# A ring of nine weight buffers and one of ten for weight sums, the mask on VectorE, a short unit in two PSUM banks, and the first wide group prepared inside the gates

## The chip, the cores and the metric

The kernel runs on one NeuronCore of a Trainium2 chip. The metric is the device time of one execution in microseconds (us). The core's engines each work through a queue of their own in program order: TensorE (PE in the rows, PEld for its weight loads), VectorE (DVE), ScalarE (ACT), GpSimd (POOL) and SyncE (SP), which issues most DMAs. An engine waits on semaphores where an instruction needs another engine's result, and everything behind that instruction on its queue waits with it.

## The reference

Three stages in float32 run after one another on 2304 tokens of width 512:

```
x = windowed_attention(q, k, v)          # 4 batches, 8 heads, 576 positions, window 64
# mixture of experts: 8 experts, hidden width 1024, the two best of each token
for e in range(8):
    for k in range(2):
        mask = top2[:, k] == e
        h = maximum(x[mask] @ w1[e], 0)
        out[mask] += top2_w[mask, k] * (h @ w2[e])
# second feed-forward network, hidden width 2048
h = x @ w_in
g = where(h >= 1, h, where(h <= -1, 0, (h + 1)**2 / 4))
return g @ w_out
```

The weights `w_in` and `w_out` of the last stage arrive as float64 and are turned into float32 on the chip.

## The kernel before

Attention and routing fill the span up to about 108 us. Then come the units of the mixture: expert 0 for all its tokens in two units (0a, 0b), experts 1 to 6 (units e1 to e6, up to 640 rows each, gathered by rank), a short unit "sp" of at most 64 rows of overflow for the last expert (513 to 534 us), and expert 7 in two units (7a, 7b). The last stage has a plain group of two token blocks (g0, 582 to 629 us) and four wide groups of four blocks, which use a Winograd scheme of seven products in place of eight.

TensorE runs one list of steps. A step (ui, f) of unit ui handles chunk f of eight: `do_mm1` of the next chunk (hidden layer, two PSUM banks, split in two parts) and `do_mm2` of its own (output layer, five banks). Every fp32 product is made of three products of a high and a low part, so each weight chunk is split: ScalarE copies the high part (`split_w`, L160), VectorE subtracts it (L161). The hidden layer leaves PSUM through ScalarE (`he`, L876) and VectorE (L879), and the next chunk's products wait until VectorE has read that bank.

Between these operations, units e1 to e6 decode the weights of the last stage. `dec_load` brings one of 32 pieces of float64, `dec_a` makes a mask of its zeros on ScalarE (L185 to L187), and `dec_b` builds float32 on VectorE (L199 to L204) and ends on GpSimd (add L206, multiplication with the mask L207). For every four pieces `sums` builds the eight weight operands of the Winograd scheme: four sums on GpSimd (L224), and eight splits by ScalarE (L240) and VectorE (L241), which then go back to DRAM (w1o). The work of `sums` is put on the list `todo` as four items, and each step takes one item. At the end of each unit GpSimd also issues five scatters of the unit's result rows (L910) and, step by step, the gathers of the next unit's rows (L840).

The short unit computes its hidden layer in one bank: four chunks, a Relu on ScalarE over them (`mm1_half`, L974), four more chunks, a second Relu.

In g0 the hidden layer goes through `act_gate`: r = Relu(h + 1) and then m = min(r/2, 1), (r - m) * m, which is the gate function. Step p of g0 has two gates, (p, 0) and (p, 1); the products of step p + 1 write the same two banks and wait for r of step p. Functions placed on `fill` run inside a gate, behind r. While g0 runs, the rows of the first wide group are read back (`prep_gather`), mixed (`prep_mix`, L1032 and L1034), transposed and copied (`xcopy`, L1232 and L1236), summed (`xsums`, L1246) and split (`xsplit`, L1255 and L1256), at places (p, j) that the last loop lists by hand, where j counts sevenths of a step's output products.

Of the kernel before, what the change touches and what calls it, by code (L numbers as in the profile page):

```python
# [33 lines left out]
RING = 10  # L34
PAIRS = (0, 1, 3, 5)
# [22 lines left out]
def fused_kernel(ctx, tc, qT, kT, v, wg, noise, wcat, out, wd=None):  # L58
# [71 lines left out]
    def stream(k, shape, dt, name):  # L130
        return ring.tile(shape, dt, tag="w", name=name) if k < 2 else pool["we"].tile(shape, dt, tag=f"w{k}", name=name)
# [21 lines left out]
    def split_w(n, half=None):  # L153
        if SP <= n < NCE:
            return
        if half in (None, 0):
            halves[n] = ring.tile([P, 2, 1024], F32R, tag="w", name=f"w{n}")
# [22 lines left out]
    def dec_a(i):  # L180
# [6 lines left out]
        nc.scalar.activation(m, m, AF.Relu)  # L187
        d64[i] = (d64[i], m)

    def dec_b(i):  # L190
        if wd is None:
            t = d64.pop(i)
        else:
# [8 lines left out]
                                           op1=ALU.bitwise_or)  # L202
            nc.vector.tensor_scalar(out=ti, in0=hw, scalar1=-0x800000, scalar2=None, op0=ALU.bitwise_and)
# [3 lines left out]
            nc.gpsimd.tensor_tensor(out=t, in0=t, in1=m, op=ALU.mult)  # L207
# [10 lines left out]
    def sums(p, ta, tb):  # L218
# [27 lines left out]
        todo.extend((lambda: (first(), cut(0, 1)), lambda: (second(), cut(5, 2)), lambda: cut(3, 6), lambda: cut(4, 7)))  # L246
# [522 lines left out]
    dec, xpc = ExitStack(), ExitStack()  # L769
# [192 lines left out]
    def mm1_half(un, n):  # L962
        f, hf = n - SP, NF // 2
        ps = un["m1"][0]
# [37 lines left out]
    unit("sp", E, 0, 1, SP, NF, None, (0,), (2, 3))  # L1002
# [97 lines left out]
    wi, wo = [], []  # L1100
# [30 lines left out]
    def plain(ui, p):  # L1131
        w = wi[p % WS]
        for f in range(2):
# [4 lines left out]
            key = units[ui]["key"]  # L1138
            mm1_of(key, n, units[ui]["T"], act_gate, units[ui]["m1"], part(0), part(1))
# [70 lines left out]
    slots, staged = [], {}  # L1210
# [15 lines left out]
    def xcopy(ui, b):  # L1226
        un = units[ui]
        t = gat.pop((un["key"], b))
        free = [x for x in bank[2:7] if x not in units[ui - 1]["m2"]]
        TR = bank[7] if b % 2 == 0 else free[b // 2 % len(free)]  # L1230
        for k in range(4):
            nc.tensor.transpose(TR[:, k * P:k * P + P], t[:, k * P:k * P + P], idn)  # L1232
        if b == 0:
# [3 lines left out]
                             TR.rearrange("p (o k t) -> p o k t", o=2, k=2), AF.Copy)  # L1237

    def xsums(ui):
        f, d = staged[ui]  # L1240
        if d:
            slots.extend(raw.tile([P, 2, 2, HT], F32R, tag="raw", name=f"xa{i}") for i in range(3))
        t1, t2, t3, t4 = d or [pool["sc"].tile([P, 2, HT], F32, tag="s", name=f"xd{ui}_{i}") for i in range(4)]
# [3 lines left out]
        staged[ui] = (b11, b21, t2, t3, t4, t1, b22)  # L1247
# [25 lines left out]
    for s in range(len(seq)):  # L1273
# [5 lines left out]
        decode = 1 < ui < E - 1 and f <= 6  # L1279
        if ui == 1 and f > 5:  # L1280
            dec_load(ndl)
            ndl += 1
# [8 lines left out]
        if ui == 1 and f == 2:  # L1291
            for x, k in (("rd", 3), ("td", 4), ("so", 6)):
                pool[x] = dec.enter_context(tc.tile_pool(name=x, bufs=k, reuse_waits="tile"))
# [65 lines left out]
        if ui == SPILL - 1 and f == 2:  # L1359
# [86 lines left out]
```

## Time and profile before

| what | value |
|---|---|
| median of 3 runs | 987.42 us (986.65 to 991.91) |
| profiled execution | 988.92 us, of which the span of the profile is 986.9 us |
| TensorE busy | 949.9 us, 96% of the span |
| VectorE, ScalarE, GpSimd busy | 653.2, 461.3, 271.9 us |
| mean granted clock of TensorE | 0.986 of full speed |

A row of the trace gives the start, the duration, the engine, the line of the kernel and the tiles that an operation writes and reads. Where an engine stood idle before it, the row ends in brackets with the idle time and the operation that ended it.

### The profile page before, as it was taken

The page shows a single profiled execution, that of the slowest core. Times are in us where ns is not written, and L with a number is a line of the kernel's source. Part 1 is how long each engine was busy: PE and PEld are TensorE (multiplying, and loading weights), DVE is VectorE, ACT ScalarE, POOL GpSimd, SP SyncE. Part 2 cuts the span into 40 slices and gives each one's busy share as a digit, 9 for nine tenths or more (in the row PEclk, how much of TensorE's full clock was granted, in tenths as well). Part 3 has the DMA queues.
Part 4 walks back from the last instruction along what each step waited for, and adds up shares of the span by engine and source line. Part 5 has one row for each costly group of instructions (what it writes and reads, how often), then busy time and mean ns, then how long its engine had stood idle before and what let it go on. Part 6 is the DMA issues. An engine that isn't in the chain of part 4 may idle for free. (4 is left out here: it accounts for less than half of the span.)

```text
span 986.9 us, 18441 instructions
## 1 busy us (share of the span) xinstructions
PE 949.9 (96%) x6918; PEld 841.7 (85%) x6918; DVE 653.2 (66%) x1358; ACT 461.3 (47%) x938; POOL 271.9 (28%) x303
## 2 busy tenths in 40 slices
PE   8998799999999999799998999899999999999998
PEld 6887789998898888698886888798899899889996
DVE  4689476576786978676442267776766777576664
ACT  6987224566566666554332254344334333433222
POOL 3221113456557676643401020112101201210000
PEclk9999999999999999999998999899999999999999
DMA  8874126568667787777736367484567458556531
GB/s 258 279 243 158 54 97 202 178 231 273 247 232 252 267 287 248 236 229 231 264 108 215 113 206 269 149 304 155 167 225 250 162 173 299 170 171 211 183 117 43
DMA packets 92796, 201.17 MB, mean 204 GB/s; under 512 B 7432, under 2 KB 17928, under 8 KB 92704
## 3 DMA queue, kind: packets, MB, share of 16 engines
q1 hardware_dynamic: 85264, 177.84, 54.1%
q0 software_dynamic: 6144, 19.76, 5.6%
q10 hardware_dynamic: 1296, 2.36, 0.6%
q8 instruction: 55, 0.90, 0.4%
q14 instruction: 37, 0.30, 0.1%
HBM read 159.65 MB, written 40.29 MB: 203 GB/s over the span
## 5 line engine op out<-in xcount | busy, mean ns | idle before, releaser
L931 PE MATMUL bank<-wo,hg 128*128 128x512 f32 x864 | 238.8, 395 | 0.0
L931 PE MATMUL bank<-w,he 128*128 128x512 f32 (+3 forms) x696 | 170.3, 396 | 0.0
L931 PEld LDWEIGHTS bank<-wo,hg 128*128 128x128 f32 x864 | 147.4, 189 | 17.2
L931 PEld LDWEIGHTS bank<-w,he 128*128 128x128 f32 (+3 forms) x696 | 124.7, 184 | 26.6
L868 PE MATMUL bank<-xhie,w 128*128 128x288 f32 (+4 forms) x768 | 123.9, 304 | 9.1 <-DVE he L879 9.0
L868 PEld LDWEIGHTS bank<-xhie,w 128*128 128x128 f32 x768 | 114.5, 192 | 16.6 <-DVE he L879 11.7
L161 DVE TENSOR_TENSOR w<-raw,w 128x1024 fp32r<-128x1024 f32 (+1 forms) x71 | 95.0, 1338 | 39.1 <-ACT w L160 37.0
L876 ACT ACTIVATE he<-bank 128x288 fp32r<-128x288 f32 (+4 forms) x96 | 40.2, 420 | 132.2 <-PE bank L868 129.7
L1176 PEld LDWEIGHTS bank<-xb,wi 128*128 128x128 f32 x576 | 82.2, 192 | 13.8 <-ACT r L886 4.2
L1176 PE MATMUL bank<-xb,wi 128*128 128x256 f32 x576 | 86.7, 287 | 3.8 <-ACT r L886 3.5
L1200 ACT ACTIVATE hg<-cg 128x512 fp32r<-128x512 f32 x64 | 40.3, 629 | 100.5 <-DVE cg L1198 100.5
L1037 POOL TENSOR_TENSOR y<-y,y 128x512 f32<-128x512 f32 x14 | 19.1, 1364 | 200.0 <-ACT y L1036 191.2
L1176 PEld LDWEIGHTS bank<-xc,wi 128*128 128x128 f32 x480 | 67.2, 188 | 7.6 <-DVE wg L1161 0.6
L1176 PE MATMUL bank<-xc,wi 128*128 128x256 f32 x480 | 70.2, 281 | 0.2 <-DVE wg L1161 0.2
L160 ACT ACTIVATE w<-raw 128x1024 fp32r<-128x1024 f32 (+1 forms) x71 | 69.3, 976 | 0.0
L868 PE MATMUL bank<-xloe,w 128*128 128x288 f32 (+4 forms) x384 | 69.2, 303 | 0.0
L879 DVE SCALAR_TENSOR_TENSOR he<-bank,he 128x320 fp32r<-128x320 f32 (+8 forms) x120 | 43.4, 400 | 31.4 <-ACT he L876 26.6
L1194 ACT ACTIVATE mg<-cg 128x512 f32<-128x512 f32 x64 | 40.1, 626 | 48.1 <-DVE cg L1166 46.3
L206 POOL TENSOR_TENSOR td<-rawd 128x512 f32<-128x512 f32 x32 | 33.3, 1042 | 94.9 <-DVE rawd L204 86.3
L1195 DVE SCALAR_TENSOR_TENSOR cg<-mg,cg 128x512 f32<-128x512 f32 x64 | 47.0, 734 | 18.8 <-ACT mg L1194 18.8
L868 PEld LDWEIGHTS bank<-xloe,w 128*128 128x128 f32 x384 | 58.6, 192 | 0.0
L1204 DVE SCALAR_TENSOR_TENSOR hg<-cg,hg 128x512 fp32r<-128x512 f32 x64 | 46.0, 718 | 9.1 <-ACT hg L1200 8.7
(302 smaller groups left out, 1635.1 us busy)
## 6 DMA issues: line engine op xcount, KB each, us to landing
wi<-w1o SPq DMA_DIRECT2D x56, 1024.0 KB
raw<-wcat SPq DMA_DIRECT2D x64, 512.0 KB
rawd<-wd SPq DMA_DIRECT2D x32, 512.0 KB
w1o<-so SPq DMA_DIRECT2D x64, 256.0 KB
y<-y_dram SPq DMA_DIRECT2D x30, 256.0 KB
vE<-v SPq DMA_DIRECT2D x18, 260.0 KB
x_dram<-x SPq DMA_DIRECT2D x18, 256.0 KB
k<-kT SPq DMA_DIRECT2D x8, 512.0 KB
```

The lines of the kernel that those rows point to most:

```text
L160: nc.scalar.activation(w[:, 0, c], t[:, c], AF.Copy)
L161: nc.vector.tensor_tensor(out=w[:, 1, c], in0=t[:, c], in1=w[:, 0, c].bitcast(F32), op=ALU.subtract)
L206: nc.gpsimd.tensor_tensor(out=t, in0=hf, in1=lf, op=ALU.add)
L868: nc.tensor.matmul(ps, lhsT=l[k], rhs=r[:, k, s:s + w], start=(c == 0), stop=(c == len(prods) - 1))
L876: nc.scalar.activation(hh, ps, AF.Relu)
L879: nc.vector.scalar_tensor_tensor(out=t, in0=ps[:, c], scalar=0.0, in1=hh[:, c].bitcast(F32), op0=ALU.max, op1=ALU.subtract)
L931: nc.tensor.matmul(M2[b][0:w], lhsT=h2[:, o:o + w], rhs=r[n], start=(first and a == 0), stop=(last and a == end))
L1176: nc.tensor.matmul(ps, lhsT=w[:, l, k * P:k * P + P], rhs=r[:, m, k, :], start=(c == 0), stop=(c == len(prods) - 1))
L1194: nc.scalar.activation(st["m"], c, AF.Relu, scale=0.5)
L1195: nc.vector.scalar_tensor_tensor(out=c, in0=st["m"], scalar=1.0, in1=c, op0=ALU.min, op1=ALU.subtract)
L1200: nc.scalar.activation(h2[:, 0:T], c, AF.Copy, scale=-1.0)
L1204: nc.vector.scalar_tensor_tensor(out=h2[:, T:2 * T], in0=c, scalar=-1.0, in1=h2[:, 0:T].bitcast(F32), op0=ALU.mult, op1=ALU.subtract)
```

## The change

The ring of split weights gets nine buffers in place of ten (the last chunk of the first expert, and one more of the later weight tiles, get places of their own), and the decode pieces are spread over the steps by a new rule. The four GpSimd sums of four pieces are issued in one item of `todo`; ScalarE and VectorE split in that item and in the next only operands that need no sum, and the summed ones two and three items behind; the buffers for it grow from six to ten. ScalarE's Relu and GpSimd's multiplication for the mask become one VectorE operation in the middle of `dec_b`. The short unit's first half leaves its bank through VectorE, and the second half has a bank of its own. `act_gate` makes half of r on ScalarE and uses combined VectorE operations; and the first wide group's mixing, copies, sums and splits move from the loop into the gates of g0.

```diff
-RING = 10
-PAIRS = (0, 1, 3, 5)
+RING = 9
+PAIRS = (0, 2, 3, 5)
+DEC = 6
...
         nc.scalar.activation(m, m, AF.Sign, bias=tiny[:, 0:1])
-        nc.scalar.activation(m, m, AF.Relu)
...
+            nc.vector.scalar_tensor_tensor(out=hf, in0=m, scalar=0.0, in1=hf, op0=ALU.max, op1=ALU.mult)
             nc.vector.tensor_scalar(out=ti, in0=hw, scalar1=-0x800000, scalar2=None, op0=ALU.bitwise_and)
...
             nc.gpsimd.tensor_tensor(out=t, in0=hf, in1=lf, op=ALU.add)
-            nc.gpsimd.tensor_tensor(out=t, in0=t, in1=m, op=ALU.mult)
...
-        todo.extend((lambda: (first(), cut(0, 1)), lambda: (second(), cut(5, 2)), lambda: cut(3, 6), lambda: cut(4, 7)))
+        todo.extend((lambda: (first(), second(), cut(0, 1)), lambda: cut(4, 7), lambda: cut(5, 2), lambda: cut(3, 6)))
...
         nc.scalar.activation(r, ps, AF.Relu, bias=1.0)
+        nc.scalar.activation(m, r, AF.Copy, scale=0.5)
         while fill:
             fill.popleft()()
-        nc.vector.tensor_scalar(out=m, in0=r, scalar1=0.5, scalar2=1.0, op0=ALU.mult, op1=ALU.min)
-        nc.vector.tensor_tensor(out=r, in0=r, in1=m, op=ALU.subtract)
-        nc.vector.tensor_tensor(out=r, in0=r, in1=m, op=ALU.mult)
-        nc.scalar.activation(hh, r, AF.Copy)
-        nc.vector.tensor_tensor(out=hl, in0=r, in1=hh.bitcast(F32), op=ALU.subtract)
+        nc.vector.scalar_tensor_tensor(out=r, in0=m, scalar=1.0, in1=r, op0=ALU.min, op1=ALU.subtract)
+        nc.vector.scalar_tensor_tensor(out=r, in0=m, scalar=1.0, in1=r, op0=ALU.min, op1=ALU.mult)
+        nc.scalar.activation(hh, r, AF.Copy, scale=-1.0)
+        nc.vector.scalar_tensor_tensor(out=hl, in0=r, scalar=-1.0, in1=hh.bitcast(F32), op0=ALU.mult, op1=ALU.subtract)
...
-        ps = un["m1"][0]
+        ps = un["m1"][f // hf]
...
-            nc.scalar.activation(hbuf["sp"][:, sl], ps[:, sl], AF.Relu)
+            if f < hf:
+                nc.vector.tensor_scalar(out=hbuf["sp"][:, sl], in0=ps[:, sl], scalar1=0.0, scalar2=None, op0=ALU.max)
+            else:
+                nc.scalar.activation(hbuf["sp"][:, sl], ps[:, sl], AF.Relu)
...
-        for out, x, y, e in ((t1, b12, b11, d), (t2, b22, t1, d), (t3, b22, b12, None), (t4, b21, t2, None)):
-            (nc.vector if e else nc.gpsimd).tensor_tensor(out=out, in0=x, in1=y, op=ALU.subtract)
...
+            (nc.vector if d else nc.gpsimd).tensor_tensor(out=out, in0=x, in1=y, op=ALU.subtract)
...
-        decode = 1 < ui < E - 1 and f <= 6
+        decode = 1 < ui < E - 1 and f < DEC and (ui, f) != (2, 0) or (ui, f) in ((2, 6), (2, 7), (3, 6))
...
+    FILL.update({(3, 0): [later(prep_mix, units[g1], b) for b in (0, 1)],
+                 (3, 1): [later(prep_mix, units[g1], b) for b in (2, 3)],
+                 (4, 0): [later(xcopy, g1, b) for b in (0, 1)],
+                 (4, 1): [later(xsplit, g1, 0)],
+                 (5, 0): [later(xsums, g1, (0, 1)), later(xsplit, g1, 1)],
+                 (5, 1): [later(xsums, g1, (2, 3))],
+                 (6, 0): [later(xsplit, g1, j) for j in (2, 3)],
+                 (6, 1): [later(xsplit, g1, j) for j in (4, 5)]})
```

The order of the products on TensorE stays as it was but for the first wide group's transposes. On GpSimd the sums move ahead of the scatters. The rows below are GpSimd's queue around the change from unit e4 to e5 in the kernel before: L206 and L207 end a decode, L910 are the scatters of e4's rows, L224 the sums.

```order
219 L224 TENSOR_TENSOR so_5_5232<-td_5162 128x256
220 L224 TENSOR_TENSOR so_2_5234<-so_5_5232,td_5009 128x256
221 L206 TENSOR_TENSOR td_5242<-rawd_5018 128x512
222 L207 TENSOR_TENSOR td_5242<-td_5242,dm_5203 128x512
223 L910 DMA y_dram<-ye_0_5282,rank_i 23040x512
...
227 L910 DMA y_dram<-ye_4_5309,rank_i 23040x512
228 L224 TENSOR_TENSOR so_3_5332<-td_5009,td_5162 128x256
229 L224 TENSOR_TENSOR so_6_5334<-td_5009,so_2_5234 128x256
230 L840 DMA xge_0_5344<-x_dram,rank_i 128x512
```

The same place in the changed kernel (L207 is its add that ends a decode, L911 its scatters):

```order
191 L911 DMA y_dram<-ye_0_5222,rank_i 23040x512
...
195 L911 DMA y_dram<-ye_4_5249,rank_i 23040x512
196 L841 DMA xge_0_5273<-x_dram,rank_i 128x512
197 L207 TENSOR_TENSOR td_5327<-rawd_4979 128x512
198 L841 DMA xge_1_5336<-x_dram,rank_i 128x512
199 L224 TENSOR_TENSOR so_5_5390<-td_5327 128x256
200 L224 TENSOR_TENSOR so_2_5392<-so_5_5390,td_5047 128x256
201 L224 TENSOR_TENSOR so_3_5394<-td_5047,td_5327 128x256
202 L224 TENSOR_TENSOR so_6_5396<-td_5047,so_2_5392 128x256
```

The four sums now stand together, with no scatters between them. VectorE reaches their splits two items later: the rows below are its queue in the changed kernel after those sums (L162 subtracts a split weight, L241 splits the operands, L199 to L205 decode a piece, L203 being the new operation with the mask).

```order
681 L162 TENSOR_TENSOR w_5473<-raw_5325,w_5473 128x1024
682 L241 TENSOR_TENSOR so_4_5478<-td_5327,so_4_5478 128x256
683 L241 TENSOR_TENSOR so_7_5481<-td_5327,so_7_5481 128x256
684 L199 TENSOR_SCALAR td_5484<-rawd_5271 128x512
685 L201 SCALAR_TENSOR_TENSOR rawd_5271<-rawd_5271,td_5484 128x512
686 L203 SCALAR_TENSOR_TENSOR rawd_5271<-dm_5448,rawd_5271 128x512
687 L204 TENSOR_SCALAR td_5484<-rawd_5271 128x512
688 L205 SCALAR_TENSOR_TENSOR rawd_5271<-rawd_5271,td_5484 128x512
...
694 L241 TENSOR_TENSOR so_5_5390<-so_5_5390 128x256
695 L241 TENSOR_TENSOR so_2_5392<-so_2_5392 128x256
```

Two splits that read only decoded pieces (td) stand ahead of the first two that read sums.

In g0, VectorE's queue in the kernel before holds five splits for the first wide group (L1256) between the gates of step 6 and of step 7 (L889 to L893 are one gate):

```order
865 L889 TENSOR_SCALAR m<-r 128x256
866 L890 TENSOR_TENSOR r<-r,m 128x256
867 L891 TENSOR_TENSOR r<-r,m 128x256
868 L893 TENSOR_TENSOR hg_85_7459<-r,hg_85_7459 128x256
869 L1256 TENSOR_TENSOR xb_7337<-xlos,xb_7337 128x512
870 L1256 TENSOR_TENSOR xb_7338<-xlos,xb_7338 128x512
871 L1256 TENSOR_TENSOR xa_7425<-xlos,xa_7425 128x512
872 L1256 TENSOR_TENSOR xa_7426<-xlos,xa_7426 128x512
873 L1256 TENSOR_TENSOR xa_7427<-xhis,xa_7427 128x512
874 L889 TENSOR_SCALAR m<-r 128x256
```

In the changed kernel (L891 to L894 are a gate's VectorE operations, L1269 the splits, L1258 the sums) the same stretch reads:

```order
879 L1258 TENSOR_TENSOR xlos<-xhis 128x512
880 L1258 TENSOR_TENSOR xlos<-xhis,xlos 128x512
881 L891 SCALAR_TENSOR_TENSOR r<-m,r 128x256
882 L892 SCALAR_TENSOR_TENSOR r<-m,r 128x256
883 L894 SCALAR_TENSOR_TENSOR hg_83_7374<-r,hg_83_7374 128x256
884 L1269 TENSOR_TENSOR xb_7290<-xlos,xb_7290 128x512
885 L1269 TENSOR_TENSOR xb_7291<-xlos,xb_7291 128x512
886 L891 SCALAR_TENSOR_TENSOR r<-m,r 128x256
887 L892 SCALAR_TENSOR_TENSOR r<-m,r 128x256
888 L894 SCALAR_TENSOR_TENSOR hg_84_7410<-r,hg_84_7410 128x256
889 L1269 TENSOR_TENSOR xa_7363<-xlos,xa_7363 128x512
890 L1269 TENSOR_TENSOR xa_7364<-xlos,xa_7364 128x512
```

Each gate now has its share of the preparation in front of its own VectorE operations.

## Rows read from the trace of the kernel before

**Rows 1.** The page: busy time, share of the span, instructions of two engines.

```profile
PE 949.9 (96%) x6918; PEld 841.7 (85%) x6918; DVE 653.2 (66%) x1358; ACT 461.3 (47%) x938; POOL 271.9 (28%) x303
```

**Rows 2.** Stretches of the span: engines' busy us, granted clock, DMA share, GB/s.

```profile
240.00:260.00 20.00, 17.68 (x94) 15.88 (x94) 13.57 (x20) 10.16 (x20) 13.60 (x12) 0.91 0.72 235
380.00:390.00 10.00, 8.79 (x58) 7.78 (x57) 7.87 (x15) 5.36 (x12) 6.97 (x6) 1.00 0.87 281
410.00:430.00 20.00, 14.78 (x73) 13.14 (x73) 8.53 (x19) 8.81 (x16) 10.94 (x11) 0.83 0.74 250
510.00:530.00 20.00, 15.26 (x176) 12.30 (x176) 6.00 (x9) 5.62 (x10) 5.21 (x5) 0.83 0.16 59
600.00:610.00 10.00, 10.00 (x67) 9.01 (x66) 7.43 (x18) 4.14 (x12) 0.00 (x0) 1.00 1.01 356
620.00:640.00 20.00, 16.30 (x89) 14.28 (x89) 13.80 (x29) 5.98 (x14) 1.48 (x2) 0.83 0.39 133
183.00:470.00 287.00, 277.78 (x1624) 249.16 (x1623) 217.62 (x364) 169.77 (x316) 166.74 (x143) 0.98 0.72 242
```

**Rows 3.** Waits of PE from 109 to 990 us: total, times, longest.

```profile
PE bank L868 <- DVE he L879: 9.0, 4, 5.2
PE bank L970 <- ACT hsp L974: 4.6, 1, 4.6
```

**Rows 4.** Timeline around 413 us, change from unit e4 to e5.

```profile
408.96 2.25 POOL L910 DMA_INDIRECT y_dram<-ye,rank_i  x1
...
416.95 0.73 POOL L224 TENSOR_TENSOR so<-td,so 128x256 f32<-128x256 f32 x1
...
417.72 0.42 DVE L241 TENSOR_TENSOR so<-so 128x256 fp32r<-128x256 f32 x1 [7.42 <-POOL so L224]
...
418.57 2.29 PE L868 MATMUL bank<-xhie,w 128*128 128x288 f32 x8 [5.22 <-DVE he L879]
```

**Rows 5.** Waits of DVE from 183 to 470 us: total, times, longest.

```profile
DVE so L241 <- POOL so L224: 20.5, 9, 7.4
```

**Rows 6.** Single lines of DVE and POOL from 183 to 470 us: ns minimum, median, maximum, or busy us and mean ns.

```profile
L161 DVE TENSOR_TENSOR w<-raw,w x40: 1206/1500/2291, 183.2 to 469.6; 128x1024 fp32r<-128x1024 f32 x40
...
L204 DVE SCALAR_TENSOR_TENSOR rawd<-rawd,td x32: 693/694/696, 185.9 to 446.3; 128x512 f32<-128x512 uint32 x32
...
L207 POOL TENSOR_TENSOR td<-td,dm 128x512 f32<-128x512 f32 x32 | 42.3, 1323 | 2.5
```

**Rows 7.** Timeline of the short unit.

```profile
518.11 1.62 PE L970 MATMUL bank<-xsp,w 128*64 128x64 f32 x48
...
519.79 1.23 DVE L161 TENSOR_TENSOR w<-raw,w 128x1024 fp32r<-128x1024 f32 x1 [0.27 <-issue]
...
523.87 0.38 ACT L974 ACTIVATE hsp<-bank 128x256 f32<-128x256 f32 x1 [4.12 <-remote]
...
524.31 3.68 PE L970 MATMUL bank<-xsp,w 128*64 128x64 f32 x64 [4.58 <-ACT hsp L974]
```

**Rows 8.** Timeline of g0 up to the first wide products.

```profile
597.87 0.37 ACT L886 ACTIVATE r<-bank 128x256 f32<-128x256 f32 x1
...
600.04 0.39 ACT L886 ACTIVATE r<-bank 128x256 f32<-128x256 f32 x1
...
604.19 1.32 ACT L1032 ACTIVATE y<-y,wts 128x512 f32<-128x512 f32 x2
...
604.93 1.42 DVE L1034 SCALAR_TENSOR_TENSOR y<-y,wts 128x512 f32<-128x512 f32 x2 [0.19 <-ACT y L1032]
...
620.77 0.69 DVE L1246 TENSOR_TENSOR xlos<-xhis,xlos 128x512 f32<-128x512 f32 x1
...
627.82 1.29 DVE L1256 TENSOR_TENSOR xa<-xlos,xa 128x512 fp32r<-128x512 f32 x2
...
628.57 0.36 ACT L886 ACTIVATE r<-bank 128x256 f32<-128x256 f32 x1
...
628.98 1.65 PE L1176 MATMUL bank<-xb,wi 128*128 128x256 f32 x6 [2.95 <-ACT r L886]
```

More of the change, by code (lines that the diff above doesn't have):

```diff
@@ L1224, in xset, with xturn, xcopy @@
         staged[ui] = (f, d)
-    def xcopy(ui, b):
+    held = {}
+    def xturn(ui, b):
         un = units[ui]
         t = gat.pop((un["key"], b))
-        free = [x for x in bank[2:7] if x not in units[ui - 1]["m2"]]
-        TR = bank[7] if b % 2 == 0 else free[b // 2 % len(free)]
+        free = [bank[7]] + [x for x in bank[2:7] if x not in units[ui - 1]["m2"]]
+        held[ui, b] = to = free[b % len(free)]
         for k in range(4):
-            nc.tensor.transpose(TR[:, k * P:k * P + P], t[:, k * P:k * P + P], idn)
+            nc.tensor.transpose(to[:, k * P:k * P + P], t[:, k * P:k * P + P], idn)
+    def xcopy(ui, b):
         if b == 0:
@@ L1236, in xcopy, with xsums @@
         nc.scalar.activation(staged[ui][0][:, h:h + 2, :, at:at + P],
-                             TR.rearrange("p (o k t) -> p o k t", o=2, k=2), AF.Copy)
-    def xsums(ui):
+                             held.pop((ui, b)).rearrange("p (o k t) -> p o k t", o=2, k=2), AF.Copy)
+    def xsums(ui, part=(0, 1, 2, 3)):
         f, d = staged[ui]
-        if d:
+        if d and 0 in part:
             slots.extend(raw.tile([P, 2, 2, HT], F32R, tag="raw", name=f"xa{i}") for i in range(3))
-        t1, t2, t3, t4 = d or [pool["sc"].tile([P, 2, HT], F32, tag="s", name=f"xd{ui}_{i}") for i in range(4)]
+        if 0 in part:
+            parts[ui] = d or [pool["sc"].tile([P, 2, HT], F32, tag="s", name=f"xd{ui}_{i}") for i in range(4)]
+        t1, t2, t3, t4 = parts[ui]
         b11, b21, b12, b22 = (f[:, i] for i in range(4))
-        for out, x, y, e in ((t1, b12, b11, d), (t2, b22, t1, d), (t3, b22, b12, None), (t4, b21, t2, None)):
-            (nc.vector if e else nc.gpsimd).tensor_tensor(out=out, in0=x, in1=y, op=ALU.subtract)
-        staged[ui] = (b11, b21, t2, t3, t4, t1, b22)
+        for i in part:
+            out, x, y = ((t1, b12, b11), (t2, b22, t1), (t3, b22, b12), (t4, b21, t2))[i]
+            (nc.vector if d else nc.gpsimd).tensor_tensor(out=out, in0=x, in1=y, op=ALU.subtract)
+        if 3 in part:
+            staged[ui] = (b11, b21, t2, t3, t4, t1, b22)
     def xsplit(ui, j):
@@ L1278, in fused_kernel @@
         last = f == len(un["ch"]) - 1
-        decode = 1 < ui < E - 1 and f <= 6
-        if ui == 1 and f > 5:
-            dec_load(ndl)
-            ndl += 1
+        decode = 1 < ui < E - 1 and f < DEC and (ui, f) != (2, 0) or (ui, f) in ((2, 6), (2, 7), (3, 6))
+        if ui == 2 and f == 0:
+            w7.close()
+            for x, k in (("rd", 3), ("td", 4), ("so", 10)):
+                pool[x] = dec.enter_context(tc.tile_pool(name=x, bufs=k, reuse_waits="tile"))
+            for _ in range(2):
+                dec_load(ndl)
+                ndl += 1
         if decode and ndl < n64:
@@ L1290, in fused_kernel @@
             choice_weights()
-        if ui == 1 and f == 2:
-            for x, k in (("rd", 3), ("td", 4), ("so", 6)):
-                pool[x] = dec.enter_context(tc.tile_pool(name=x, bufs=k, reuse_waits="tile"))
+        if ui == SPILL - 1 and f == 2:
+            assert not todo and not stores
+            dec.close()
+            pool["we"] = ffn.enter_context(tc.tile_pool(name="we", bufs=1, reuse_waits="tile"))
         if ui == U7A and f == 0:
@@ L1400, in fused_kernel @@
                     prep_gather(nxt, 2 * p + j)
[L1401 to L1404 removed]
+                if not late:
+                    if 1 <= p < 3 and j in (2, 4):
+                        prep_mix(nxt, 2 * (p - 1) + j // 2 - 1)
+                    if 2 <= p < 4 and j in (1, 3):
+                        xturn(ui + 1, 2 * (p - 2) + j // 2)
+                        xcopy(ui + 1, 2 * (p - 2) + j // 2)
+                elif (p, j) in ((2, 5), (2, 6), (3, 0), (3, 1)):
+                    xturn(ui + 1, 2 * (p - 2) + (j - 5 if p == 2 else j))
+                elif p == 3 and j in (3, 4):
+                    xcopy(ui + 1, j - 1)
                 for x in AT[late].get((p, j), ()):
```

27 lines of the change are left out of this document (12 added, 15 removed).

## Prediction

> **What bounds the kernel now.** I read the page first: TensorE is busy for 949.9 of 986.9 us [rows 1]. What is left to gain is its 37 us of idle time and the stretches in which its clock is low. The change leaves TensorE's products as they are, so I price only those two things. Next I read stretch by stretch [rows 2]. The reader is to see that idle time and low clock come together: 240 to 260 (2.3 us idle, clock 0.91), 410 to 430 (5.2 idle, 0.83), 510 to 530 (4.7 idle, 0.83), 620 to 640 (3.7 idle, 0.83). Then I read TensorE's waits [rows 3]: 9.0 us in four waits for VectorE's `he`, and 4.6 us in one for the short unit's Relu. Attention's own idle time, before 109 us, is untouched.
>
> **Sums behind scatters.** The timeline shows the largest wait from its root [rows 4]. GpSimd begins five scatters at 408.96; the sums queued behind them end at about 417.7; VectorE has stood idle for 7.42 us for the first split of a sum; `he` stands behind that split, and TensorE waits 5.22 us for `he`. In the decode units VectorE waits so nine times, 20.5 us in all [rows 5]. In the change GpSimd does all four sums in one run, and the splits of summed operands come two and three steps later; a step is about 7 us (287 us for 40 splits of weights, one in a step [rows 2, 6]). Against that stands the time of scatters and sums, 417.7 - 408.96 = 8.7 us. I went through the eight groups of pieces in the new order: wherever a split could still meet the scatters in time, it is one that reads decoded pieces alone. So of the 9.0 us I take out the waits of 5.22 us [rows 4], 2.32 (240 to 260) and 1.21 (380 to 390 [rows 2]), behind each of which VectorE stands idle for such a sum: **-8.75**. The fourth, 0.25, stays.
>
> With them goes the low clock. [...] In the second stretch part of the low time lay inside the wait itself, where it costs nothing; I take 2.7 there and 1.7 in the first: **-4.4**. Bounds: 0, if the waits stay, and 5.2.
>
> **Mask on VectorE.** One more operation of 128x512 with two inputs, like L204 (0.694 us), 32 times: +22.2 us of VectorE. GpSimd loses 42.3 us (L207), ScalarE a Relu [rows 6]. From 183 to 470 VectorE is busy for 217.6 of 287 us [rows 2]; with the new operation it would be 239.8, or 84%. That mean hides the full steps: I add up what VectorE has to do in a step with a decode, splits and a transposed block and come to about 6.6 us now and 7.3 us then, an estimate, against a step's 7.2, less in the units with fewer rows. A step that runs over borrows from the next; only when about 4 us have been borrowed does TensorE wait (an estimate: more than half of a step's products lie between a chunk's `he` and the next need of its bank). Six decode steps in a row at 0.5 over borrow 3 us, and two steps without a decode give it back. So I charge **+0.5**; bounds 0 and +9 (rivals).
>
> One thing makes VectorE cheaper again: L161 takes 1.21 us at its shortest and 1.50 in the median, up to 2.29, in the stretch in which GpSimd computes [rows 6]. [...]
>
> **Ring of nine, pieces spread.** With nine buffers a split takes the slot of a chunk whose last product precedes products that the same engine waits for anyway; no wait is added. Loads of pieces move by a step on SyncE's queue and have a step of slack. 0.
>
> **Short unit.** ScalarE's Relu on the first half starts at 523.87, and the second half's 64 products follow at 524.31, after a wait of 4.58 us, because they write the same bank [rows 7]. With a bank of its own the second half starts at once. VectorE's eviction stands behind L161, which ends at about 521.0, so hsp is ready at 521.4, while 64 products of 34 ns (48 in 1.62) run until 521.9: hidden. Gain 4.58 of wait. At full clock the 64 products take 2.2 us instead of 3.68, 1.5 less, and the following ones about 0.7: 2.2 of the 3.4 that the clock row would allow [rows 2, 7]. Less 0.5 for handing over: **-6.3**. One thing is unexplained: the last product of the first half should be done by about 519.8, and yet ScalarE got its signal only at 523.8. If VectorE gets it as late, the output products wait for hsp until 524.2, about 2.3 us. Bounds -2.5 and -7.2.
>
> **Gates.** A gate takes 2.03 to 2.17 us from r to r now (597.87 to 600.04 [rows 8]), and TensorE does not wait but for the last: r of step 7 comes at 628.57 and the wide products wait 2.95. In the change a gate has as many operations in a row as before (m on ScalarE, two on VectorE, hg), so I take 2.1. But what is filled in stands behind r and ahead of the gate's own VectorE operations, and hg and the next r stand behind those. From r of gate (3, 0), 600.04, to r of gate (7, 0) there are eight gates: 16.8 us. The fills add VectorE's work: four mixings of 0.71, four sums of 0.69, six splits of 0.65, 9.5 us in all [rows 8]; and ScalarE's part ahead of it, about 0.65 in each of five fills, 3.3, and handoffs of about 0.1, 1.2 together: 14. Mixing blocks 2 and 3 inside gate (3, 1) also comes some 6 us earlier than now, while the DMA engines are full (share 1.01 in 600 to 610 [rows 2]): up to 1.5 us of waiting for the loads, half of it taken. Sum: 600.04 + 16.8 + 14 + 0.8 = 631.6, against 628.57 now, **+3.0**. TensorE has no work to put there: its own list ends where it ends now. The low clock at 628 to 636 stays. What it gains is one less contended sum (the other three take 0.69 when GpSimd does none). Bounds: -6.4, if all fills are hidden, and +5.
>
> **Sum.** -8.75 - 4.4 + 0.5 - 6.3 + 3.0 = -15.95. From the profiled execution, 988.92, that is 973.0; it lies 1.5 above the median of the runs, so **971.5**. Its own range is 967 to 977.
>
> **The rivals.**
>
> (a) The fills are hidden: what the gates wait for overlaps more than I allow. Then 2.95 and 0.75 of waits and 2.7 of clock go, -6.4 instead of +3.0: 962. Against it: all of it is on two queues in program order.
>
> (b) The short unit's signal is late again: 3.8 of the 6.3 are not gained, 975.3.
>
> (c) VectorE becomes the bound of the decode units. The stretches in which it is nearly full already speak for it. If a step runs 1 us over, six borrow 6, 2 more than the 4 that are free; over the five units 9 us, in waits spread too thin to lower the clock: 980.
>
> (d) Slower than before: the new operation is held up by GpSimd's sums and adds each time, by a whole 1.0 us beside its 0.69. A step is then 1.7 over, six borrow 10, TensorE waits 6 in each of five units, 30 us, less what is gained: 971.5 + 30 = 1001. The point from which this decides is a step 1.4 us longer than TensorE's. Against it: L204 at 693 to 696 ns next to it [rows 6].
>
> (e) The split does not do what it says, since GpSimd is late by more than two steps: 13 us stay, 984.
>
> **How the numbers follow.** Chances: the forecast 0.54, (a) 0.10, (b) 0.10, (c) 0.15, (d) 0.05, (e) 0.06. The range goes from (a) to just past (c), **962 to 982**, and leaves out (d), (e) and the far end of (c). 0.5% is about 5 us: faster is below 982.5. Forecast, (a), (b) and most of (c) are faster, 0.85; (e) and the rest of (c) the same, 0.09; (d) and mishaps slower, 0.06.
>
> **What would show it.** No wait of VectorE for `so` from GpSimd over 1 us, and no clock below 0.95 in the stretches of 240 to 260 and 410 to 430. L161's median below 1.50 us. No wait at the short unit's second half, its 64 products in about 2.2 us. In g0, waits of TensorE for r of steps 5 to 7, and the first wide products 32 us after r of gate (3, 0) instead of 28.9. The forecast is wrong if TensorE waits for `he` at the ends of decode runs, or if the gates' r come every 2.8 us or faster through step 6, which is TensorE's own pace.

## The result and the profile after

The changed kernel takes 976.06 us in the median of four runs (975.29 to 977.03), beside 987.83 (986.65 to 991.91) for the kernel before: ratio 0.9874, 95% interval 0.9844 to 0.9904. The profiled execution takes 975.29 us with a span of 973.5, so 13.4 us less span than before. The forecast was 971.5 with a range of 962 to 982; of the 15.95 us that it took off, 11.8 came off in the medians.

To see where the time went I take from both traces the start of the first product of each stage; the differences of these starts are the stages' lengths. The right pair (before_again and after_again below) was profiled later, on the chip that is called the third below.

| stage, from its first product to the next one's | before | after | before_again | after_again | forecast |
|---|---|---|---|---|---|
| up to e1 | 171.1 | 172.8 | 172.9 | 170.8 | 0 |
| e1 to e6 (decode) | 342.6 | 331.1 | 343.1 | 330.9 | -12.65 |
| short unit | 18.4 | 15.1 | 12.2 | 11.8 | -6.3 |
| 7a, 7b | 49.8 | 49.8 | 49.8 | 49.8 | 0 |
| g0 and the first four wide products | 54.9 | 54.4 | 54.8 | 56.6 | +3.0 |
| the rest | 350.1 | 350.3 | 350.1 | 350.2 | 0 |

The first row is code of which the change touches only the ring of weight buffers, in expert 0's units; it moves by about 2 us between the two profiles of either kernel, in opposite directions, which is the noise in which the others are read.

TensorE's waits after, from 109 to 990 us (total, times, longest), answer to [rows 3]:

```profile
PE bank L1181 <- ACT r L887: 3.1, 2, 2.6
PE bank L971 <- issue: 2.2, 6, 0.4
PE bank L869 <- DVE he L880: 1.6, 3, 1.2
PE bank L869 <- ACT r L887: 1.6, 2, 0.9
```

The 9.0 us for `he` have become 1.6. The 4.6 for the short unit's Relu have become 2.2 in which TensorE waits for nothing that the profile shows. The waits for r have grown from 4.1 to 4.7 us; in the kernel before they were

```profile
PE bank L1176 <- ACT r L886: 3.5, 2, 3.0
PE bank L868 <- ACT r L886: 0.6, 2, 0.4
```

VectorE's waits (175 to 465 us) have no entry for a sum any more, where it was 20.5 us [rows 5]. The stretches that answer to [rows 2] (engines' busy us, granted clock, DMA share, GB/s):

```profile
240.00:260.00 20.00, 18.66 (x106) 16.20 (x105) 19.49 (x31) 9.91 (x20) 13.38 (x12) 1.00 0.89 299
410.00:430.00 20.00, 19.83 (x122) 17.59 (x121) 17.97 (x30) 10.84 (x22) 8.95 (x10) 1.00 0.57 187
600.00:620.00 20.00, 15.35 (x91) 13.22 (x90) 14.23 (x30) 10.74 (x26) 0.00 (x0) 0.93 0.48 157
183.00:470.00 287.00, 285.27 (x1689) 255.61 (x1688) 233.89 (x401) 152.92 (x289) 124.84 (x118) 1.00 0.75 253
```

Around the old waits the clock is at full speed. From 183 to 470 TensorE is busy for 285.3 of 287 us. GpSimd is down from 166.7 to 124.8, and VectorE up by 16.3, not by the 22.6 of the added operation (L203). The lines that answer to [rows 6] (ns minimum, median, maximum; or busy us and mean ns):

```profile
L162 DVE TENSOR_TENSOR w<-raw,w x41: 1210/1226/1751, 182.8 to 462.6; 128x1024 fp32r<-128x1024 f32 x41
...
L203 DVE SCALAR_TENSOR_TENSOR rawd<-dm,rawd 128x512 f32<-128x512 f32 x32 | 22.6, 707 | 1.1
```

The split of weights is back near its shortest time: 1.23 us in the median, 1.50 before.

### The profile page after: what moved, and what is told of

It reads as the page before. It is cut to its first block, busy times and chain, and to the rows that moved or that the text cites. A ratio compares the mean times of both kernels' runs of the same rounds, so it can differ in the third digit from the quotient of the medians.

```text
span 973.5 us, 18334 instructions
## 1 busy us (share of the span) xinstructions
PE 946.0 (97%) x6918; PEld 837.8 (86%) x6918; DVE 661.0 (68%) x1377; ACT 447.0 (46%) x921; POOL 218.9 (22%) x269
## 4 chain that ended last, share of the span: by engine, by line
PE 81%; DVE 8%; ACT 5%; issue 3%; DMA 2%; SPq 0%; POOL 0%; another core or an unknown queue 0%; DVEq 0%; POOLq 0%; ACTq 0%
PE bank L932 37%; PE bank L869 20%; PE bank L1181 16%; PE bank L748 1%; PE bank L364 1%; PE ob L401 1%; ACT p L380 1%; DVE mx L371 1%; PE bank L387 1%; DMA y<-y_dram 1%; PE bank L421 1%; DMA w1o<-so 1%; PE bank L439 1%; PE bank L971 1%; PE bank L1239 1%
## 5 line engine op out<-in xcount | busy, mean ns | idle before, releaser
L869 PE MATMUL bank<-xhie,w 128*128 128x288 f32 (+4 forms) x768 | 121.0, 299 | 1.8 <-DVE he L880 1.6
L869 PEld LDWEIGHTS bank<-xhie,w 128*128 128x128 f32 x768 | 112.0, 188 | 8.9 <-DVE he L880 3.0
L162 DVE TENSOR_TENSOR w<-raw,w 128x1024 fp32r<-128x1024 f32 (+1 forms) x71 | 82.0, 1156 | 32.6 <-ACT w L161 26.7
L1181 PEld LDWEIGHTS bank<-xb,wi 128*128 128x128 f32 x576 | 81.1, 190 | 13.4 <-ACT r L887 3.8
L207 POOL TENSOR_TENSOR td<-rawd 128x512 f32<-128x512 f32 x32 | 33.3, 1040 | 133.5 <-DVE rawd L205 78.0
```

The lines of the kernel that those rows point to most:

```text
L162: nc.vector.tensor_tensor(out=w[:, 1, c], in0=t[:, c], in1=w[:, 0, c].bitcast(F32), op=ALU.subtract)
L207: nc.gpsimd.tensor_tensor(out=t, in0=hf, in1=lf, op=ALU.add)
L869: nc.tensor.matmul(ps, lhsT=l[k], rhs=r[:, k, s:s + w], start=(c == 0), stop=(c == len(prods) - 1))
L1181: nc.tensor.matmul(ps, lhsT=w[:, l, k * P:k * P + P], rhs=r[:, m, k, :], start=(c == 0), stop=(c == len(prods) - 1))
```

## The experiments

Theory A, the forecast's: VectorE was late because sums stood behind scatters on GpSimd's queue; the new order cures it, and the mask is a cost. Rival B: GpSimd simply had too much to do; taking the mask from it is the cure. The order rows ahead set a limit to Theory A: at the change from e4 to e5 the new sums do not move ahead of the scatters but stand behind them, with a decode and two gathers between; what is new there is that VectorE's splits of them come two items later. For the short unit and the gates the questions were whether the bank and the fills do what was worked out. The first four experiments ran on one chip (before: 990.26 us), the next four on a second (982.92), the last four on a third (981.30); ratios are to the kernel before on the same chip. Which chip the first two profiles (before and after) ran on is not known. The expectations give totals at the level of those first profiles, so across chips the ratios and the lengths of stages are to be compared, not the totals.

**One bank (one_bank).**

```diff
-        ps = un["m1"][f // hf]
+        ps = un["m1"][0]
...
-            if f < hf:
-                nc.vector.tensor_scalar(out=hbuf["sp"][:, sl], in0=ps[:, sl], scalar1=0.0, scalar2=None, op0=ALU.max)
-            else:
-                nc.scalar.activation(hbuf["sp"][:, sl], ps[:, sl], AF.Relu)
+            nc.scalar.activation(hbuf["sp"][:, sl], ps[:, sl], AF.Relu)
...
-    unit("sp", E, 0, 1, SP, NF, None, (0, 1), (2, 3))
+    unit("sp", E, 0, 1, SP, NF, None, (0,), (2, 3))
```

> The changed kernel with the short unit as before: one bank, both halves through ScalarE. From the short unit's first product to unit 7a's first one the changed kernel took 15.1 us and the kernel before 18.4. Mine: the bank wait is back, 18.4 again, so 3.3 us more than the changed kernel, about 979.3. Rival: what was gained there was not the bank but where the rest put the unit in time; then 15 to 16 us and no change of the total.

980.03 us, ratio 0.9903 (0.9887 to 0.9920); the short unit takes 17.6 us, not the 18.4 of the kernel before, and TensorE waits for the Relu again:

```profile
514.72 3.54 PE L971 MATMUL bank<-xsp,w 128*64 128x64 f32 x64 [4.72 <-ACT hsp L975]
```

The other three kernels on this chip have the second bank and take 16.4, 15.3 and 16.3 us there (old_sums, old_spread, old_mask), the changed kernel 15.1 in its first profile. So where TensorE is held up, the bank is worth 1.2 to 2.5 us of the unit, not 6.3; in the total it is not clear of the noise (0.9903 against the changed kernel's 0.9874, with intervals that overlap).

**Sums in the old order (old_sums), pieces in the old spread (old_spread), both (old_both).**

```diff
-        todo.extend((lambda: (first(), second(), cut(0, 1)), lambda: cut(4, 7), lambda: cut(5, 2), lambda: cut(3, 6)))
+        todo.extend((lambda: (first(), cut(0, 1)), lambda: (second(), cut(5, 2)), lambda: cut(3, 6), lambda: cut(4, 7)))
...
-        decode = 1 < ui < E - 1 and f < DEC and (ui, f) != (2, 0) or (ui, f) in ((2, 6), (2, 7), (3, 6))
+        decode = 1 < ui < E - 1 and f <= DEC and (ui, f) != (2, 0) or (ui, f) == (2, 7)
```

> The changed kernel with the sums issued and split in the old order (two and two, splits of sums in the next item); the new spread of pieces, the ten buffers and the mask stay. From e1's first product to the short unit's first one the changed kernel took 331.1 us, the kernel before 342.6. Mine: the order is what counts, since a split then reads a sum of the same step; VectorE waits for sums again and 5 to 11 us come back, 981 to 987 in all. Rival: the new spread alone keeps the sums off the scatters, or the relief of GpSimd by the mask does; then under 2 us, 976 to 978.

> The changed kernel with the pieces spread nearly as before: seven steps of each unit up to the fifth decode and the last unit the rest; the new order of the sums stays. Mine: the order suffices, 331 to 333 us for the decode units, 976 to 978 in all. Rival: the spread is what keeps sums and scatters apart, and with seven decode steps in a row in the units with fewer rows VectorE overruns; 4 to 8 us more, 980 to 984.

> The changed kernel with both the old order of the sums and nearly the old spread of the pieces; the mask stays on VectorE. With either of the two undone alone the decode units took 331.8 and 330.8 us (331.1 in the changed kernel, 336.4 with the mask back on GpSimd, 342.6 in the kernel before). Theory now: GpSimd's time is the cause and the mask is the larger cure; without its 1.3 us a piece the old order costs little, 332 to 335 us, 976 to 980 in all. Rival, the forecast's: sums queued behind five scatters are late whatever the mask costs, and one of order or spread is needed; then the wait of 5 us at one change of units comes back with its low clock, 338 us or more, 982 or more.

Decode units: 331.8, 330.8 and 333.5 us; in all 976.95 (ratio 0.9872, 0.9845 to 0.9900), 974.57 (0.9838, 0.9820 to 0.9856) and 973.24 (0.9906, 0.9884 to 0.9927). Either part can be undone for nothing, and both together cost about 2.5 us of the units: a wait of 2.1 us for `he` comes back at the change from e4 to e5, and the low clock behind it (0.91 from 400 to 420 us). My expectation for old_sums, 5 to 11 us, failed: the order that I had seen as the cure is hardly needed.

**Mask back on GpSimd (old_mask).**

```diff
+        nc.scalar.activation(m, m, AF.Relu)
...
-            nc.vector.scalar_tensor_tensor(out=hf, in0=m, scalar=0.0, in1=hf, op0=ALU.max, op1=ALU.mult)
...
             nc.gpsimd.tensor_tensor(out=t, in0=hf, in1=lf, op=ALU.add)
+            nc.gpsimd.tensor_tensor(out=t, in0=t, in1=m, op=ALU.mult)
```

> The changed kernel with the mask as before: a Relu on ScalarE and a multiplication on GpSimd (32 times 1.3 us), no operation on VectorE. Mine: TensorE hardly sees it, 330 to 333 us for the decode units and 975 to 978 in all; the median of the weight split's VectorE part goes back from 1.23 to about 1.5 us, so VectorE is not freed by the 22 us taken off it. Rival 1: VectorE was near its bound, and with 0.69 us less a step the remaining 1.6 us of waits for he go: 974. Rival 2: GpSimd is late again for the sums: 980 or more.

982.82 us (979.57 to 985.10), ratio 0.9925 (0.9902 to 0.9948). TensorE's waits from 165 to 505 us, VectorE's split and the stretch of the decode units in this run:

```profile
PE bank L870 <- DVE he L881: 3.3, 3, 2.2
PE bank L933 <- issue: 3.2, 4, 0.8
```

```profile
L162 DVE TENSOR_TENSOR w<-raw,w x40: 1216/1518/2786, 190.3 to 465.1; 128x1024 fp32r<-128x1024 f32 x40
```

```profile
183.00:470.00 287.00, 282.11 (x1673) 252.73 (x1672) 231.99 (x367) 172.71 (x320) 175.11 (x150) 1.00 0.72 249
```

Here VectorE has 22.6 us less to do than in the changed kernel, and is busy for 232.0 us against 233.9. Its operations take longer by nearly what was taken off it: the split's median is 1.52 us again, with a longest of 2.79. Taken one by one, the 13 of these 40 splits with no GpSimd sum, add or multiplication beside them take 1.23 us each, the 27 others 1.22 to 2.79, 20 of these the median of 1.52 or more. The kernel before has the same picture: 15 of its 40 splits have no such operation beside them and take 1.22 to 1.23 us, the 25 others 1.21 to 2.29, 21 of these 1.49 or more. So in both traces no split that stands alone is lengthened, and most that have GpSimd beside them are; what lengthens them is not shown. The decode units take 336.4 us. In 3.2 of these TensorE waits four times for nothing that the profile shows (467 to 473 us; more on that below); without them it would be 333.2, 2 us above the changed kernel, an estimate. My expectation of 330 to 333 us and 975 to 978 in all failed. Rival 2's total came, 980 or more, but not by its cause: VectorE does not wait for a sum once in this run, and most of the rest of the total lies in the pauses, in the short unit (16.3 us) and in g0 (56.7).

**The mask alone (before_mask).** The kernel before, with the three lines of the mask of the change and nothing else.

> The kernel before with the mask alone moved to VectorE (no Relu on ScalarE, no multiplication on GpSimd); sums, spread, ring, short unit and gates as before. Theory now: GpSimd's time on the pieces is a cause of the late sums by itself, so the decode units go from 342.6 to 333 to 337 us, and 6 to 10 us come off the total. Rival, the forecast's: the mask only adds work to VectorE and the sums stay behind the five scatters; 342 us or more, and a total that is the same or slower.

972.98 us, ratio 0.9912 (0.9892 to 0.9931). The changed kernel on the same chip has 972.88 and 0.9905 (0.9880 to 0.9931). The decode units take 331.5 us, not 343.1: the mask alone gives 11.6 of the 12.2 us that the change gives there, more than my 333 to 337, and in the total these three lines do as much as the whole change. The rows show how: the stretch of the decode units, the waits of TensorE (109 to 985 us) and of VectorE (175 to 465 us), and the timeline at the change from e4 to e5, as in [rows 4], behind the row of the kernel before with which that place begins.

```profile
183.00:470.00 287.00, 284.42 (x1688) 255.40 (x1687) 229.00 (x404) 153.21 (x289) 121.06 (x119) 1.00 0.75 255
```

```profile
PE bank L867 <- DVE he L878: 2.5, 2, 2.1
```

```profile
DVE so L240 <- POOL so L223: 10.3, 6, 4.4
```

```profile
406.38 1.04 POOL L206 TENSOR_TENSOR td<-rawd 128x512 f32<-128x512 f32 x1 [2.67 <-ACT ye L940]
```

```profile
400.61 1.04 POOL L206 TENSOR_TENSOR td<-rawd 128x512 f32<-128x512 f32 x1 [3.68 <-DVE rawd L204]
...
401.81 1.01 POOL L909 DMA_INDIRECT y_dram<-ye,rank_i  x1 [0.16 <-issue]
...
408.75 0.72 POOL L223 TENSOR_TENSOR so<-td,so 128x256 f32<-128x256 f32 x1
...
409.51 0.43 DVE L240 TENSOR_TENSOR so<-so 128x256 fp32r<-128x256 f32 x1 [4.45 <-POOL so L223]
...
410.35 1.33 PE L867 MATMUL bank<-xhie,w 128*128 128x288 f32 x8 [2.07 <-DVE he L878]
```

The sums still stand behind five scatters, and VectorE still waits for them, but 4.45 us where it was 7.42. From the start of the add that ends the decode to the first scatter GpSimd takes 1.20 us (400.61 to 401.81) where it took 2.58 (406.38 to 408.96), since the multiplication is gone, and the first scatter takes 1.01 us, not 2.25. The edit also takes the Relu off ScalarE (153.2 us busy, 169.8 before), and no run parts the two; at this wait, GpSimd's own two rows account for 2.6 of the 3.0 us. TensorE waits 2.07 where it was 5.22, and behind 2.07 the clock stays at full speed here. The other three of the four waits shrink to 0.4 or nothing, and the low clock goes with them: 9.0 + 4.4 (the forecast's own estimate for the clock) becomes 2.5.

**Gates and preparation as before (old_gates).** `act_gate`, the list AT, `xcopy`, `xsums` and the places in the last loop as in the kernel before, all else as changed.

> The changed kernel with the gate and the first wide group's preparation as before. From g0's first product to the first product with xa the changed kernel took 54.4 us, the kernel before 54.9. Mine: the two orders cost about the same, 54 to 56 us, so 975.5 to 977.5 in all. Rival: the new fills cost 3 us, as the forecast had it, and g0 gets shorter by that, 973.

969.41 us, ratio 0.9874 (0.9851 to 0.9897); g0 and the first wide products 54.6 us. Kernels with the new gates take 54.4 to 56.7 there (54.4 and 56.6 in the changed kernel's two profiles, 56.6 in short4 on the same chip as this run), those with the old ones 54.6 to 55.6, so the fills gain nothing and cost up to 2 us. My expectation for the stage, 54 to 56, held.

**The fills behind the gate's two operations (fill_behind).**

```diff
         nc.scalar.activation(m, r, AF.Copy, scale=0.5)
-        while fill:
-            fill.popleft()()
         nc.vector.scalar_tensor_tensor(out=r, in0=m, scalar=1.0, in1=r, op0=ALU.min, op1=ALU.subtract)
         nc.vector.scalar_tensor_tensor(out=r, in0=m, scalar=1.0, in1=r, op0=ALU.min, op1=ALU.mult)
+        while fill:
+            fill.popleft()()
```

> The changed kernel with the fills run behind the gate's two VectorE operations instead of ahead of them; all else stays. Mine: ScalarE's part of a fill then runs while VectorE makes the gate's two operations, and VectorE's part while ScalarE makes hg, so a gate with a fill takes about 2.5 to 2.9 us from r to r instead of 3.3 to 4.1, which is TensorE's own 2.8; the waits for r of 0.7, 0.9 and 2.6 us go, and the low clock behind the last: 4 to 6 us less, 970 to 972. Rival: the chain is bound by VectorE's sum of work, whatever its order; then under 1.5 us less, 974.5 or more.

964.78 us (963.26 to 965.99), ratio 0.9813 (0.9794 to 0.9832); g0 and the first wide products 49.8 us: 6.8 less than in short4 on the same chip, 4.6 less than in the changed kernel's first profile, where I had expected 4 to 6. The timeline at gates (6, 0) and (6, 1), which hold two splits each, then TensorE's waits from 560 to 630 us and the stretch of 600 to 620:

```profile
600.37 0.39 ACT L887 ACTIVATE r<-bank 128x256 f32<-128x256 f32 x1 [0.32 <-PE bank L869]
...
601.11 1.14 ACT L1268 ACTIVATE xb<-xlos 128x512 fp32r<-128x512 f32 x2
...
602.15 0.42 ACT L893 ACTIVATE hg<-r 128x256 fp32r<-128x256 f32 x1
...
602.48 0.37 ACT L887 ACTIVATE r<-bank 128x256 f32<-128x256 f32 x1
```

```profile
PE bank L1181 <- ACT sg L1162: 0.6, 1, 0.6
PE bank L1239 <- DVE y L1038: 0.5, 1, 0.5
PE bank L1181 <- ACT r L887: 0.2, 1, 0.2
```

```profile
600.00:620.00 20.00, 19.16 (x132) 17.28 (x132) 14.71 (x33) 9.66 (x23) 0.00 (x0) 1.00 0.59 189
```

ScalarE's 1.14 us of splits now lie in the time in which it would have waited for VectorE's two operations; from r to r it takes 2.11 us with this fill, as gates without one do in this run (2.09 to 2.14). r no longer waits for its own queue but for TensorE (0.32 us at gate (6, 0)), and the clock is full (1.00 from 600 to 620).

**Four chunks ahead (short4), and both kernels again (before_again, after_again).**

```diff
-        while ndone < min(s + (NF - f if ui == SPILL and f < NF - 1 else 2), len(seq)):
+        while ndone < min(s + (5 if ui == SPILL - 1 and last else NF - f if ui == SPILL and f < NF - 1 else 2), len(seq)):
```

> The changed kernel with the first four chunks of the short unit's hidden layer put ahead of unit e6's last output products instead of one ahead and three behind. In all runs so far VectorE or ScalarE gets the first half's signal 5.7 to 5.9 us after the 48 small products begin, and 0.8 to 1.0 us after the last of e6's five scatters on GpSimd. Theory A: the burst of small products delays the signal; then it comes 6 us or more after the burst begins here too, behind the output products or in their midst, the four products' worth of pauses in the second half go or move, and the unit gets shorter by 1 to 3 us, 973 to 975. Theory B: the scatters, or what goes with them, hold TensorE's signals; then the signal of the first half comes within 0.3 us of its last product, since no scatter runs yet, and the pauses stay in the second half behind the output products; no more than 1 us less.

> The kernel before, profiled once more. On the chip of the first profiles TensorE's small products of the short unit were held up for about 4 us in all of five kernels; on the chip of the second four experiments in none, and the kernel before took 982.9 there instead of 987 to 990. If this chip is like the second: the short unit takes 14 to 15 us instead of 18.4, and its wait for the Relu under 1.5 us instead of 4.6; the decode units take 342 to 343 us as before. If like the first: 18.4 again.

> The changed kernel, profiled once more on the chip of the run above. Decode units 330.5 to 331.5 us, g0 and the first products of the wide group 54 to 55. Short unit 11.8 us on a chip like the second, 15 to 16.4 on one like the first. In all 12 to 15 us less than the kernel before, ratio 0.985 to 0.988.

short4: 971.70 us, ratio 0.9881 (0.9859 to 0.9904), short unit 12.0 us. It can't decide between its two theories, since in none of the runs on this chip was there a delay: old_both, with the changed kernel's short unit, ran it in 11.7 us with its 112 small products in one piece. before_again (984.93 us in its one run) has 12.2 there, less than the 14 to 15 expected, after_again (972.88, ratio 0.9905, 0.9880 to 0.9931) 11.8. Two parts of the expectation for after_again failed: g0 and the first wide products take 56.6 us, not 54 to 55, and the total is 8.4 us below the median of the kernel before on this chip (981.30), not 12 to 15. The short unit of the changed kernel in its first profile, with the stretch around it, and of the kernel before on the third chip answer to [rows 7]:

```profile
508.28 1.61 PE L971 MATMUL bank<-xsp,w 128*64 128x64 f32 x47
...
513.18 0.36 PE L971 MATMUL bank<-xsp,w 128*64 128x64 f32 x5 [0.36 <-issue]
513.91 1.43 PE L971 MATMUL bank<-xsp,w 128*64 128x64 f32 x41 [0.38 <-issue]
514.00 0.42 DVE L976 TENSOR_SCALAR hsp<-bank 128x256 f32<-128x256 f32 x1 [2.83 <-remote]
```

```profile
500.00:520.00 20.00, 17.31 (x203) 13.50 (x202) 6.42 (x10) 5.23 (x9) 5.20 (x5) 1.00 0.26 88
```

```profile
520.39 1.62 PE L970 MATMUL bank<-xsp,w 128*64 128x64 f32 x48
522.12 0.38 ACT L974 ACTIVATE hsp<-bank 128x256 f32<-128x256 f32 x1
...
522.56 2.09 PE L970 MATMUL bank<-xsp,w 128*64 128x64 f32 x64 [0.54 <-ACT hsp L974]
```

On the third chip the signal of the first half comes as soon as its products are done, the bank costs 0.54 us, and the 64 products behind it take 33 ns each (2.09 us), no longer than the 34 of the 48 before (1.62).

**Both in one (best).** fill_behind and short4 together.

> The changed kernel with the fills behind the gate's two VectorE operations and the first four chunks of the short unit ahead of unit e6's last output products. Against the changed kernel of this chip: 5 to 6 us less by the gates, and by the short unit nothing on a chip like the second, 1 to 3 us on one like the first.

964.53 us (964.40 to 966.95), ratio 0.9822 (0.9803 to 0.9841): the same as fill_behind within the intervals, and 8.4 us less than the changed kernel on this chip, where I had expected 5 to 6. Of those that ran, the version to take is fill_behind; the kernel before with the mask and these fills alone was not run.

## Why the prediction was right in sum and wrong in its parts

**Sums behind scatters, -8.75 and -4.4 of clock.** The size held: -11.5 in the first pair and -12.2 in the second against -12.65 with the mask's charge. The waits, their root and the clock that goes with them were read rightly. The 4.4 is an estimate from the clock rows of the kernel before: 0.09 of the 20 us from 240 to 260 is 1.8 us of full clock (1.7 was taken), and 0.17 of those from 410 to 430 is 3.4, less 0.7 inside the wait (0.87 from 413.3 to 418.5). No run shows this term by itself; what the runs showed is a clock of 1.00 in both stretches after the change, and decode units shorter by the sums above. That the new order takes the waits away is only one of two ways, and the change would not have needed it: with the mask on VectorE and the old order the units take 0.6 to 2.6 us more (before_mask 331.5, old_sums 331.8, old_both 333.5), not 11.

**Mask on VectorE, +0.5.** This step failed. It weighed VectorE's added 22.2 us only against its own splits getting faster. Both happened (the operation takes 22.6 us, 0.707 in the mean, and the split's median went from 1.50 to 1.23) and nearly cancelled: VectorE's busy time with the mask on either engine is 232.0 and 233.9. What I did not price is the other side of the move. VectorE waited for GpSimd's sums and TensorE for VectorE, and with 42.3 us off GpSimd's queue the largest of those waits is shorter by about 3 us (7.42 to 4.45 on VectorE, 5.22 to 2.07 on TensorE), the others are 0.4 or gone, and no low clock follows (1.00 from 183 to 470 us in before_mask). By itself the mask gives 11.6 us of the decode units (343.1 to 331.5), everything else in them (new sums, spread and ring) about 9.9 without it (343.1 to 333.2, an estimate: old_mask ran on another chip, and its four pauses are counted out), both together 12.2. Neither adds much to the other, which one undoing at a time could not have shown for order and spread: it took old_both and before_mask.

**Ring and spread, 0.** For the spread it held: 330.8 us with the old one. No run undoes the ring alone; before_mask has the old ring and the old spread together, and its 331.5 us leave 0.6 for both and the sums.

**Short unit, -6.3.** Mis-sized, and for a reason that was in sight. I noted that the first half's signal came 4 us after its last product could be done, set that aside as unexplained, and sized the gain as if the bank caused all of the 4.58 us. Where the signal is not late, it causes 0.54 (before_again). With the delay the changed kernel still gets its signal late (514.00, 5.7 us after the burst began at 508.28, as in the kernel before), and gains 3.3 in its first profile because the second half may run in pauses meanwhile and the clock stays up (1.00 from 500 to 520, and the 41 products behind the pauses take 35 ns each); in old_sums and old_mask, with the same code, the products behind the pauses take 59 and 60 ns each (41 and 40 in 2.42 us), about the 58 that the kernel before took at a clock of 0.50 (64 in 3.68, 524.3 to 528), and the unit takes 16.4 and 16.3. Rival (b) described the late signal, with a gain of 2.5. Without the delay the whole part is worth 0.45 (12.2 to 11.8).

**Gates, +3.0.** The mechanism was right, the size less than half. r of gate (3, 0) and the waits that follow, in the changed kernel:

```profile
586.59 0.37 ACT L887 ACTIVATE r<-bank 128x256 f32<-128x256 f32 x1
...
592.26 1.49 ACT L1036 ACTIVATE y<-y,wts 128x512 f32<-128x512 f32 x2 [0.82 <-DMA y<-y_dram]
...
605.67 1.21 PE L869 MATMUL bank<-xhig,wi 128*128 128x256 f32 x8 [0.71 <-ACT r L887]
...
612.39 1.22 PE L869 MATMUL bank<-xhig,wi 128*128 128x256 f32 x8 [0.87 <-ACT r L887]
...
616.31 0.36 ACT L887 ACTIVATE r<-bank 128x256 f32<-128x256 f32 x1
...
616.72 1.23 PE L1181 MATMUL bank<-xb,wi 128*128 128x256 f32 x6 [2.65 <-ACT r L887]
```

The load waits 0.82 as allowed for; TensorE waits for r of steps 5, 6 and 7 in turn. From r of (3, 0) to the first wide product it is 30.1 us, where I had 32.0 and the kernel before has 28.9. So the chain is 1.2 longer, not 3.0: the fills took 12.9 us (29.7 from r to r less 16.8), not 14.8. The rest of the stage gives it back or not with the clock: the two profiles of the changed kernel differ by 2.2 us in this stage, and the 20 us around the last wait read, in after and in after_again,

```profile
605.00:625.00 20.00, 15.38 (x92) 13.43 (x93) 12.62 (x27) 8.76 (x22) 0.00 (x0) 0.91 0.37 124
```

```profile
605.00:625.00 20.00, 15.57 (x91) 13.95 (x90) 11.77 (x26) 6.60 (x17) 0.00 (x0) 0.83 0.41 141
```

By the estimate above a clock of 0.91 costs 1.8 us of full clock there and one of 0.83 costs 3.4, so the forecast's "the low clock stays" held in one profile and not in the other. fill_behind shows that the step's reading of the queue was the useful part: with nothing ahead of the two operations, TensorE's waits for r go from 4.7 us to 0.2.

That the total came out as near as it did is in part luck. In the first pair the short unit gained 3.0 us less than its term and the gates cost 3.5 less, which cancel; what is left of the miss is 1.15 us of the decode units and 1.6 that the first part of the kernel happened to lose. On the third chip the same change is worth 8.4 us in the medians, about half of the 15.95 of the sum, since there the short unit has nearly nothing to give and g0 gets longer by 1.8 us.

## What to carry to other kernels

When an operation moves between engines, price both ends: the engine that is waited for may gain more than the other loses (here 42.3 us off GpSimd for 22.6 on VectorE, and 11.6 off the decode units), and an engine whose operations are stretched while its neighbour works does not get busier by the full length of what it takes over (here by 16.3 of 22.6 us). Work that is filled into a chain of dependent operations belongs into the gap in which its engine waits for the other one, not ahead of the operation that the chain needs next (here 49.8 us in place of 56.6 for the stage). A wait whose signal comes later than its cause can explain is not yet understood, and its removal must not be booked in full (here 4.58 us were booked, and 0.54 were there without the delay); a second chip may settle it.

## What the runs showed of the hardware that was not expected

In the first two profiles and in all four on the first experiments' chip TensorE was held up for about 4 us behind a burst of 48 products of 64 columns (34 ns apart). In the kernel before, the burst's signal reached ScalarE 5.7 us after it began instead of 1.7; in the changed kernel the products behind it came about five at a time, 0.73 us apart (508.28 to 513.91), while the profile shows no wait for another engine. old_mask, on that chip, has four like pauses of 0.8 us in the middle of ordinary products as well. On the other two chips none of the eight profiles has it, and six of these have the burst at the same place. It always ended 0.8 to 1.0 us after the last of five scatters; burst and scatters stand in a fixed distance, and the run that would have parted them (short4) fell on a chip without it. Since the same scatters run at the same distance on the other two chips, they are not the cause by themselves. Its cause stays open.

TensorE's granted clock fell to half behind the waits of 2.32 and 5.22 us in the kernel before (0.50 from 250 to 253 and from 419 to 423 us). It did not behind 2.07 in before_mask, but it did behind a wait of the same length at the same place in old_both. The rows from 400 to 420 us, first before_mask, then old_both:

```profile
400.00:420.00 20.00, 17.93 (x109) 15.95 (x108) 14.82 (x30) 10.70 (x20) 11.51 (x11) 1.00 0.79 272
```

```profile
400.00:420.00 20.00, 17.92 (x100) 16.06 (x99) 13.26 (x27) 10.65 (x20) 10.43 (x11) 0.91 0.79 268
```

So at about 2.1 us the length of the wait does not decide by itself, and no run shows what does. With the forecast's estimate of 2.7 us for the clock, the wait of 5.22 us cost about 8.
